# First gate weights on ScalarE's queue, and where the opening transposes of a fused attention and gated-MLP kernel stand

## The chip, the cores and the metric

The kernel runs on one core of one Trainium2 chip. The metric is the device time of one execution in microseconds. The profile's own span, from its first to its last instruction, is about 1.8 us shorter.

## The reference

With x of 2048 rows and 640 columns, everything in bfloat16:

```python
xn = _layernorm(x, axis=-1)
s = _A_ref(xn, A_k_cache, A_v_cache, A_wq, A_wo)   # 32 heads of 192, attention over the last 512 cached keys
g = _silu(_B_ref(xn, B_w_gate, B_w_up, B_w_down))  # (sigmoid(xn @ w_gate) * (xn @ w_up)) @ w_down, inner width 1536
return x + s * g
```

The change touches the first 20 us only: the normalisation of the first four row tiles (128 rows each) and the first four of the twelve column blocks of w_gate (wg) and w_up (wu).

## The kernel before

These are the parts that the change and the argument touch. VectorE computes a tile's statistics and normalises it. TensorE transposes it into PSUM in five blocks of 128 columns, and ScalarE copies the blocks into `xnT`. Only then can TensorE multiply that tile by the weights. Each PSUM buffer, `bank[i]`, is 128 x 2 x 512 float32, so 4 KiB per partition.

```python
bank = [psum.tile([P, 2, 512], F32, name=f"bank{i}") for i in range(4)]
# ... (cut)
        nc.vector.memset(warm[:], 0.0)
        load_x(0, 1)                                  # all loads on SyncE's queue
        load_x(1, 1)
        for f0, f1 in ((0, 4), (4, 8), (8, NF)):
            load_f(nc.sync, wg_sb, wg_r, f0, f1)
            load_f(nc.sync, wu_sb, wu_r, f0, f1)
            if f0 == 0:
                load_x(2, 1)
                load_x(3, 1)
# ... (cut)
        def stats_end(t):
            # ... (cut)
            if t == 0:
                nc.scalar.activation(rstd[:], mv[:, 1:2], AF.Sqrt, bias=eps_t[:], scale=1.0)
                nc.scalar.activation(junk[:], eps_t[:], AF.Sigmoid)
                stats_half(1, 0)                      # needs row tile 1, before row tile 0 is finished
                nc.vector.reciprocal(rstd[:], rstd[:])
# ... (cut)
        def turn_pe(t, c0, c1, bk, eng):
            pT = bk[:, 0:NCD * H2].bitcast(BF16).rearrange("p (c n) -> p c n", c=NCD)
            for c in range(c0, c1):
                nc.tensor.transpose(pT[:, c, :], ln[t][:, c * P:(c + 1) * P], ident[:])
            dst = xnT[:, 0, c0:c1, t * P:(t + 1) * P]
            if eng is nc.vector:
                nc.vector.tensor_copy(dst, pT[:, c0:c1, :])
            else:
                nc.scalar.activation(dst, pT[:, c0:c1, :], AF.Copy)
# ... (cut)
        def tile_gates(t, amid):                      # four groups of wg, then four of wu, five matmuls each
            # ... (cut)
            k = t % 3
            for half, w in ((0, wg_sb), (1, wu_sb)):
                for f in range(FT):
                    if (half, f) == (1, 2) and amid is not None:
                        turn_pe(amid, 0, NCD, bank[3][:, amid % 2, :], nc.scalar)
                    for c in range(NCD):
                        nc.tensor.matmul(bank[k][:, half, f * P:(f + 1) * P],
                                         lhsT=w[:, c, f * P:(f + 1) * P], rhs=xnT[:, 0, c, r],
                                         start=(c == 0), stop=(c == NCD - 1))
            # ... sigmoid on ScalarE, product on VectorE (cut)
# ... (cut)
        dummy(20)                                     # matmuls on zeros, while x is on its way
        full_stats(0)
        normal(0, ((0, 3 * P), (3 * P, D)))
        turn_pe(0, 0, 3, bank[3][:, 0, :], nc.vector)
        turn_pe(0, 3, NCD, bank[2][:, 0, :], nc.scalar)
        dummy(2)
        stats_half(1, 1)
        stats_end(1)
        normal(1)
        full_stats(2)
        tile_gates(0, 1)
        normal(2)
        full_stats(3)
        tile_gates(1, 2)
        normal(3)
        tile_gates(2, 3)
        tile_gates(3, None)
```

The softmax here doesn't subtract the row's maximum and nothing guards it: scores larger than these inputs give would overflow.

Of the kernel before, what the change touches and what calls it, by code (L numbers as in the profile page):

```python
# [8 lines left out]
AF = mybir.ActivationFunctionType  # L9
ALU = mybir.AluOpType  # L10
BF16 = mybir.dt.bfloat16
# [4 lines left out]
def kernel(  # L16
# [13 lines left out]
    nc = tc.nc  # L30
    P = 128
    H2 = 64
# [16 lines left out]
    NCD = D // P  # L49
    NF = F // P  # L50
# [19 lines left out]
    bank = [psum.tile([P, 2, 512], F32, name=f"bank{i}") for i in range(4)]  # L70
# [4 lines left out]
    ident = const.tile([P, P], BF16, name="ident")  # L75
# [5 lines left out]
    xnT = pers.tile([P, NB, NCD, TB], BF16, name="xnT")  # L81
# [5 lines left out]
    wg_r = B_w_gate.rearrange("(c p) f -> p c f", p=P)  # L87
    wu_r = B_w_up.rearrange("(c p) f -> p c f", p=P)
# [45 lines left out]
    with ExitStack() as bctx:  # L134
# [5 lines left out]
        wg_sb = wB.tile([P, NCD, F], BF16, name="wg_sb")  # L140
        wu_sb = wB.tile([P, NCD, F], BF16, name="wu_sb")
# [4 lines left out]
        def load_x(t, n):  # L146

            x = xpool.tile([P, n, D], BF16, name=f"x_sb{n}", bufs=4 if n == 1 else 2)
            nc.sync.dma_start(x[:], xf[t * P:(t + n) * P, :].rearrange("(q p) d -> p q d", p=P))  # L149
            for i in range(n):  # L150
                xt[t + i] = x[:, i, :]

        def load_f(eng, w, r, f0, f1):
            eng.dma_start(w[:, :, f0 * P:f1 * P], r[:, :, f0 * P:f1 * P])  # L154

        nc.vector.memset(warm[:], 0.0)
        load_x(0, 1)
        load_x(1, 1)
        for f0, f1 in ((0, 4), (4, 8), (8, NF)):
            load_f(nc.sync, wg_sb, wg_r, f0, f1)  # L160
            load_f(nc.sync, wu_sb, wu_r, f0, f1)
            if f0 == 0:
                load_x(2, 1)
                load_x(3, 1)
        load_x(TQ, TQ)
        nc.sync.dma_start(wd_sb[:], wd_r)
        load_x(2 * TQ, TQ)
# [7 lines left out]
        def dummy(n):  # L175
            for _ in range(n):
                nc.tensor.matmul(bank[2][:, 1, 0:256], lhsT=warm[:, 0:P], rhs=warm[:, 0:256],
                                 start=True, stop=True)

        ln = {}  # L180

        def stats_half(t, i):
            if i == 0:
                ln[t] = bwork.tile([P, 2, nc.vector.BN_STATS_DIM], F32, name="st")
            nc.vector.bn_stats(ln[t][:, i, :], xt[t][:, i * (D // 2):(i + 1) * (D // 2)])

        def stats_end(t):
            mv = bwork.tile([P, nc.vector.BN_AGGR_DIM], F32, name="mv")
            rstd = bwork.tile([P, 1], F32, name="rstd")
            nc.vector.bn_aggr(mv[:], ln[t][:])  # L190
# [3 lines that stand above are left out]
                stats_half(1, 0)  # L194
                nc.vector.reciprocal(rstd[:], rstd[:])
            else:
                nc.vector.tensor_scalar(rstd[:], mv[:, 1:2], eps, None, op0=ALU.add)
                nc.gpsimd.tensor_tensor(rstd[:], rstd[:], mhalf[:], ALU.pow)
            ln[t] = mv, rstd

        def normal(t, parts=((0, D),)):
            mv, rstd = ln[t]
            xn = xpool.tile([P, D], BF16, name="xn")
            for d0, d1 in parts:
                nc.vector.tensor_scalar(xn[:, d0:d1], xt[t][:, d0:d1], mv[:, 0:1], rstd[:, 0:1],
                                        op0=ALU.subtract, op1=ALU.mult)
            ln[t] = xn

        def turn_pe(t, c0, c1, bk, eng):
            pT = bk[:, 0:NCD * H2].bitcast(BF16).rearrange("p (c n) -> p c n", c=NCD)  # L210
            for c in range(c0, c1):
                nc.tensor.transpose(pT[:, c, :], ln[t][:, c * P:(c + 1) * P], ident[:])  # L212
            dst = xnT[:, 0, c0:c1, t * P:(t + 1) * P]
            if eng is nc.vector:
                nc.vector.tensor_copy(dst, pT[:, c0:c1, :])
            else:
                nc.scalar.activation(dst, pT[:, c0:c1, :], AF.Copy)  # L217

        def turn_dma(t):
            q = t % TQ  # L220
# [2 lines left out]
        hT = {}  # L223
# [41 lines left out]
        FT = 4  # L265

        def tile_gates(t, amid):

            if 0 not in hT:
                hT[0] = hpool.tile([P, NF, TB], BF16, name="hT")  # L270
            k = t % 3
            r = slice(t * P, (t + 1) * P)
            for half, w in ((0, wg_sb), (1, wu_sb)):
                for f in range(FT):
                    if (half, f) == (1, 2) and amid is not None:
                        turn_pe(amid, 0, NCD, bank[3][:, amid % 2, :], nc.scalar)
                    for c in range(NCD):
                        nc.tensor.matmul(bank[k][:, half, f * P:(f + 1) * P],  # L278
                                         lhsT=w[:, c, f * P:(f + 1) * P], rhs=xnT[:, 0, c, r],
                                         start=(c == 0), stop=(c == NCD - 1))  # L280
            sig = bwork.tile([P, TB], BF16, name="sig")
            nc.scalar.activation(sig[:], bank[k][:, 0, :], AF.Sigmoid)
            nc.vector.tensor_tensor(hT[0][:, 0:FT, r],
                                    bank[k][:, 1, :].rearrange("p (f n) -> p f n", f=FT),
                                    sig[:].rearrange("p (f n) -> p f n", f=FT), ALU.mult)

        def full_stats(t):
            stats_half(t, 0)
            stats_half(t, 1)
            stats_end(t)  # L290

        dummy(20)
        full_stats(0)
        normal(0, ((0, 3 * P), (3 * P, D)))
        turn_pe(0, 0, 3, bank[3][:, 0, :], nc.vector)
        turn_pe(0, 3, NCD, bank[2][:, 0, :], nc.scalar)
        dummy(2)
        stats_half(1, 1)
        stats_end(1)
        normal(1)  # L300
        full_stats(2)
        tile_gates(0, 1)
        normal(2)
        full_stats(3)
        tile_gates(1, 2)
        normal(3)
        tile_gates(2, 3)
        tile_gates(3, None)
        k = 1
        for f in range(FT, NF):  # L310
            gated(0, f, k, norm_piece(1, f - FT))
            k = (k + 1) % 4
        for b in range(1, NB):
            for f in range(2):
                gated(b, f, k)
                k = (k + 1) % 4
            for q in range(TQ):
                down(b - 1, q, k)
                k = (k + 1) % 4
            if b == 1:  # L320
                load_x(3 * TQ, TQ)
            for f in range(2, NF):
                gated(b, f, k, norm_piece(b + 1, f - 4) if b + 1 < NB and f >= 4 else None)
                k = (k + 1) % 4
# [4 lines left out]
        for q in range(TQ):  # L329
            down(NB - 1, q, k)  # L330
            k = (k + 1) % 4
# [12 lines left out]
        for m in range(DJ):  # L344
# [3 lines left out]
            k = (k + 1) % 4  # L348
# [168 lines left out]
```

## Time and profile before

| quantity | value |
|---|---|
| time, median of 3 runs | 931.99 us (931.9 to 932.08) |
| span of the profiled run | 930.2 us |
| first gate matmul | 6.94 us |
| first wu matmul | 8.69 us |
| first 512-column gate matmul (end of the opening) | 18.53 us |

In the views PE is TensorE, PEld its weight loads, DVE is VectorE and ACT is ScalarE. The first view is the table of stretches: for each stretch, its length, then the busy time and the number of instructions of PE, PEld, DVE, ACT and POOL (GpSimd), TensorE's granted clock, the busy share of the DMA engines and GB/s.

```profile
7.00:18.50 11.50, 10.33 (x176) 9.79 (x175) 5.79 (x15) 3.58 (x6) 1.67 (x3) 1.00 1.09 353
18.50:915.00 896.50, 896.50 (x7765) 527.11 (x7763) 447.14 (x696) 297.25 (x318) 123.92 (x142) 1.00 0.36 77
```

TensorE is busy through the whole stretch from 18.5 to 915 us. So nothing that the change does before 18.5 us can hide later: the end of the kernel moves with the end of the opening.

The second view is the timeline of TensorE's matmuls: start, length, line, result and operands, how often, and in brackets the idle time before it and what ended it. A matmul of 128 columns is shown 0.22 us long (the profile models where a matmul ends), but the next one starts 0.056 us later. So a gap is read from start to start: a group of 20 fills 1.12 us.

```profile
5.43 0.74 PE L212 MATMUL bank<-ident,xn 128*128 128x128 bf16 x5
...
6.94 1.28 PE L278 MATMUL bank<-xnT,wg_sb 128*128 128x128 bf16 x20
8.69 0.73 PE L278 MATMUL bank<-xnT,wu_sb 128*128 128x128 bf16 x10 [0.47 <-DMA wu_sb<-in_B_w_up_dram]
9.25 0.44 PE L212 MATMUL bank<-ident,xn 128*128 128x128 bf16 x5
9.53 0.72 PE L278 MATMUL bank<-xnT,wu_sb 128*128 128x128 bf16 x10
10.49 1.28 PE L278 MATMUL bank<-xnT,wg_sb 128*128 128x128 bf16 x20 [0.23 <-ACT xnT L217]
...
18.53 1.24 PE L231 MATMUL bank<-xnT,wg_sb 128*128 128x512 bf16 x5
```

The group of 20 that starts at 6.94 has issued its last matmul by 8.06, and wu starts at 8.69. So 0.64 us is lost to the landing of wu. The second ten of wu start at 9.53, and the next tile at 10.49 and not at 10.09: 0.40 us from start to start is lost to the copy of the five transposed blocks (0.36 us by the weight loads). The weight loads show the same gaps more plainly, since each is shown only 0.10 us long. This is the view of waits for them between 6.9 and 18.6 us: total, times, longest. "issue" means that a load stood behind a matmul that waited.

```profile
PEld L278 <- issue: 1.1, 3, 0.4
PEld L278 <- DMA wu_sb<-in_B_w_up_dram: 0.6, 1, 0.6
```

### The profile page before, as it was taken

The numbers are of one execution on the slowest core, as the hardware profiler recorded it, in microseconds if no ns is written. First come the engines' busy times: TensorE is split into PE (matmuls) and PEld (weight loads), VectorE is DVE, ScalarE is ACT, GpSimd is POOL, SyncE is SP. The second block draws the span as 40 slices with busy tenths as digits, with TensorE's granted clock in tenths as the row PEclk, the third lists the DMA queues.
The fourth block names the chain that finished last, engine by engine and source line by source line (L and its number), as shares of the span: only waits on it lengthen the run. The fifth ranks groups of instructions, "written<-read, shape, count | busy, mean of one in ns | idle before, by whom it ended". The sixth has DMA issues, their size and how long they took to land.

```text
span 930.2 us, 18111 instructions
## 1 busy us (share of the span) xinstructions
PE 922.3 (99%) x8036; PEld 546.3 (59%) x8036; DVE 467.5 (50%) x738; ACT 304.5 (33%) x330; POOL 126.5 (14%) x154
## 2 busy tenths in 40 slices
PE   8999999999999999999999999999999999999997
PEld 6445455566655666655566655566666666666665
DVE  5452522454544544554554455445555555445657
ACT  3222222433333333333333333333333333333341
POOL 1000010400010002000200020002000205565000
PEclk9999999999999999999999999999999999999999
DMA  9310420616223433433343433263327234522223
GB/s 314 83 22 8 112 61 1 195 36 138 59 52 78 105 83 61 77 83 99 67 78 58 122 69 78 54 127 69 78 47 133 69 69 78 92 63 63 52 65 102
DMA packets 157807, 76.69 MB, mean 82 GB/s; under 512 B 140784, under 2 KB 151648, under 8 KB 157728
## 3 DMA queue, kind: packets, MB, share of 16 engines
q1 hardware_dynamic: 149904, 46.56, 25.4%
q0 software_dynamic: 7248, 28.38, 10.8%
q8 instruction: 63, 1.03, 0.5%
q10 hardware_dynamic: 576, 0.59, 0.2%
q14 instruction: 16, 0.13, 0.1%
HBM read 39.45 MB, written 2.62 MB: 45 GB/s over the span
## 4 chain that ended last, share of the span: by engine, by line
PE 97%; DVE 1%; DMA 1%; ACT 0%; SPq 0%; issue 0%; DVEq 0%
PE bank L390 22%; PE bank L427 21%; PE bank L407 19%; PE bank L372 18%; PE bank L231 10%; PE bank L243 6%; PE bank L278 1%; DMA wu_sb<-in_B_w_up_dram 1%; PE bank L340 1%; DVE gate L436 1%; DVE o_sb L431 1%; ACT xnT L217 0%; PE bank L212 0%; SPq L149 0%; SPq L154 0%
## 5 line engine op out<-in xcount | busy, mean ns | idle before, releaser
L376 ACT ACTIVATE E<-bank 128x1024 bf16<-128x1024 f32 x256 | 257.9, 1023 | 477.4 <-PE bank L372 453.5
L390 PE MATMUL bank<-xnT,wq_sb 64*128 64x512 bf16 x1860 | 231.4, 376 | 0.0
L427 PE MATMUL bank<-wo_sb,oT 128*128 128x512 bf16 (+1 forms) x1536 | 228.6, 299 | 0.0
L372 PE MATMUL bank<-qT,kT 64*128 64x512 bf16 x1536 | 202.2, 377 | 0.0
L407 PE MATMUL bank<-vbuf,E 128*128 128x193 bf16 x2048 | 191.0, 247 | 0.0
L407 PEld LDWEIGHTS <-E 128*128 128x128 bf16 x2048 | 167.8, 98 | 24.2 <-issue 13.6
L397 DVE CAST qT<-bank 128x1024 bf16<-128x1024 f32 x93 | 113.9, 1224 | 132.8 <-PE bank L390 132.8
L427 PEld LDWEIGHTS <-oT 128*128 128x128 bf16 x1536 | 121.1, 98 | 76.9 <-issue 0.4
L390 PEld LDWEIGHTS <-wq_sb 64*128 64x128 bf16 x1860 | 97.2, 100 | 104.6
L372 PEld LDWEIGHTS <-kT 64*128 64x128 bf16 x1536 | 72.9, 94 | 90.1 <-issue 8.8
L413 DVE TENSOR_TENSOR o_st<-bank,rden 128x768 bf16<-128x768 f32 x128 | 122.5, 957 | 4.4
L442 DVE TENSOR_TENSOR acc<-bank,acc 128x640 f32<-128x640 f32 x96 | 79.1, 824 | 43.8 <-PE bank L427 43.8
L395 DVE COPY seen<-bank 128x2 f32<-128x2 f32 x93 | 14.8, 159 | 93.9 <-PE bank L390 93.8
L412 DVE RECIPROCAL rden<-bank 128x4 f32<-128x4 f32 x128 | 23.3, 182 | 71.4 <-PE bank L407 71.4
L231 PE MATMUL bank<-xnT,wg_sb 128*128 128x512 bf16 x220 | 54.7, 379 | 0.0
L231 PE MATMUL bank<-xnT,wu_sb 128*128 128x512 bf16 x220 | 54.7, 379 | 0.0
L243 PE MATMUL bank<-wd_sb,hT 128*128 128x512 bf16 (+1 forms) x384 | 52.8, 299 | 0.0
L237 DVE TENSOR_TENSOR hT<-bank,sig 128x512 bf16<-128x512 f32 x44 | 30.3, 689 | 43.7 <-ACT sig L234 43.7
L234 ACT ACTIVATE sig<-bank 128x512 bf16<-128x512 f32 x44 | 26.3, 597 | 68.4 <-PE bank L231 63.8
L106 POOL DMA_DIRECT2D vbuf<-in_A_v_cache_dram x28 | 20.9, 748 | 184.9 <-PE bank L407 184.9
L243 PEld LDWEIGHTS <-hT 128*128 128x128 bf16 x384 | 29.6, 98 | 23.2
L231 PEld LDWEIGHTS <-wu_sb 128*128 128x128 bf16 x220 | 21.5, 98 | 26.0
(50 smaller groups left out, 277.6 us busy)
## 6 DMA issues: line engine op xcount, KB each, us to landing
wo_sb<-in_A_wo_dram POOLq DMA_DIRECT2D x8, 960.0 KB, 7.4
wq_sb<-in_A_wq_dram POOLq DMA_DIRECT2D x7, 960.0 KB, 6.3
k_st<-in_A_k_cache_dram POOLq DMA_DIRECT2D x7, 768.0 KB, 8.0
vbuf<-in_A_v_cache_dram POOLq DMA_DIRECT2D x28, 192.0 KB, 3.0
row<-in_A_x_dram POOLq DMA_DIRECT2D x16, 160.0 KB, 2.6
oT<-o_st SPq DMA_TRANSPOSE x128, 2.6
wg_sb<-in_B_w_gate_dram SPq DMA_DIRECT2D x3, 640.0 KB, 7.4
wu_sb<-in_B_w_up_dram SPq DMA_DIRECT2D x3, 640.0 KB, 8.5
```

Of the source, the lines that this page charges most:

```text
L231: nc.tensor.matmul(bank[k][:, half, 0:r1 - r0], lhsT=w[:, c, f * P:(f + 1) * P], rhs=xnT[:, b, c, r0:r1], start=(c == 0), stop=(c == NCD - 1))
L234: nc.scalar.activation(sig[:, 0:r1 - r0], bank[k][:, 0, 0:r1 - r0], AF.Sigmoid)
L237: nc.vector.tensor_tensor(hT[b][:, f, r0:r1], bank[k][:, 1, 0:r1 - r0], sig[:, 0:r1 - r0], ALU.mult)
L243: nc.tensor.matmul(wide(k)[:, d0:d1], lhsT=hT[b][:, f, q * P:(q + 1) * P], rhs=wd_sb[:, f, d0:d1], start=(f == 0), stop=(f == NF - 1))
L372: nc.tensor.matmul(bank[k][:, i, :], lhsT=kT[r, pr, j, c * P:(c + 1) * P], rhs=q[r, pr * DJ + j, :], start=(j == 0), stop=(j == DJ - 1))
L376: nc.scalar.activation(E[u, pr][:, c, :, :], bank[k][:], AF.Exp, scale=scale_qk)
L390: nc.tensor.matmul(bank[k][:, half, :], lhsT=wq[r, c, col:col + DJ * (P - 1) + 1:DJ], rhs=xnT[r, b, c, :], start=(c == 0 and not second), ...
L397: nc.vector.tensor_copy(qT[u][:, 2 * m:2 * m + 2, :], bank[k][:])
L407: nc.tensor.matmul(o4[:, q, 0:DH + 1], lhsT=e[:, c, h % 2, q * P:(q + 1) * P], rhs=v[:, h, c, 0:DH + 1], start=(c == 0), stop=(c == KC - 1))
L413: nc.vector.tensor_tensor(o_st[u][:, :, h * DH:(h + 1) * DH], o4[:, :, 0:DH], rden[:].to_broadcast([P, TQ, DH]), ALU.mult)
L427: nc.tensor.matmul(wide(k)[:, d0:d1], lhsT=oT[u][:, cc, q * P:(q + 1) * P], rhs=wo[:, cc, d0:d1], start=(cc == 0), stop=(cc == GC - 1))
L442: nc.vector.tensor_tensor(acc[:, t, :], wide(k)[:, 0:D], acc[:, t, :], ALU.add)
```

## The change

The change means to bring the first weights sooner and to shorten the waits for copies. wg goes on ScalarE's queue, beside three rows of x on SyncE's. A clear of two of its columns makes that load wait for VectorE. The transposes of a tile stand later, before the last one or two groups of wu. They leave PSUM in two parts (three blocks, then two), both on ScalarE. The statistics of tiles 2 and 3 move forward on VectorE, and each of these tiles is normalised before the gate product that it used to follow. There are 22 dummy matmuls for 20. The diff, cut to its core:

```diff
         nc.vector.memset(warm[:], 0.0)
+        nc.vector.memset(wg_sb[:, 0, 0:2], 0.0)
         load_x(0, 1)
         load_x(1, 1)
-        for f0, f1 in ((0, 4), (4, 8), (8, NF)):
+        load_x(2, 1)
+        load_f(nc.scalar, wg_sb, wg_r, 0, 4)
+        load_f(nc.sync, wu_sb, wu_r, 0, 4)
+        load_x(3, 1)
+        for f0, f1 in ((4, 8), (8, NF)):
             load_f(nc.sync, wg_sb, wg_r, f0, f1)
             load_f(nc.sync, wu_sb, wu_r, f0, f1)
-            if f0 == 0:
-                load_x(2, 1)
-                load_x(3, 1)
# ... (cut)
-        def turn_pe(t, c0, c1, bk, eng):
+        def turn_pe(t):
+            engs = (nc.vector, nc.scalar) if t == 0 else (nc.scalar, nc.scalar)
+            for i, (c0, c1) in enumerate(((0, 3), (3, NCD))):
+                bk = bank[3][:, t % 2, :] if t or i == 0 else bank[2][:, 0, :]
# ... transposes c0 to c1 into bk, then one copy of them by engs[i] (cut)
# ... in tile_gates(t, amid): (cut)
-                    if (half, f) == (1, 2) and amid is not None:
-                        turn_pe(amid, 0, NCD, bank[3][:, amid % 2, :], nc.scalar)
+            for f in range(FT):
+                if amid == f:
+                    turn_pe(t + 1)
+                one(1, wu_sb, f, 0, NCD)
# ... (cut)
-        dummy(20)
-        full_stats(0)
+        dummy(22)
+        stats_half(0, 0)
+        stats_half(0, 1)
+        stats_end(0)
         normal(0, ((0, 3 * P), (3 * P, D)))
-        turn_pe(0, 0, 3, bank[3][:, 0, :], nc.vector)
-        turn_pe(0, 3, NCD, bank[2][:, 0, :], nc.scalar)
+        turn_pe(0)
         dummy(2)
         stats_half(1, 1)
         stats_end(1)
+        stats_half(2, 0)
         normal(1)
-        full_stats(2)
-        tile_gates(0, 1)
+        stats_half(2, 1)
+        stats_end(2)
+        stats_half(3, 0)
+        stats_half(3, 1)
         normal(2)
-        full_stats(3)
-        tile_gates(1, 2)
+        stats_end(3)
+        m0 = tile_gates(0, 3)                          # m0() is the product on VectorE
+        m0()
         normal(3)
-        tile_gates(2, 3)
-        tile_gates(3, None)
+        m1 = tile_gates(1, 2)
+        m1()
+        m2 = tile_gates(2, 2)
+        m2()
+        m3 = tile_gates(3, None)
+        m3()
```

More of the change, by code (lines that the diff above doesn't have):

```diff
@@ L207, in normal @@
             ln[t] = xn
-        def turn_pe(t, c0, c1, bk, eng):
-            pT = bk[:, 0:NCD * H2].bitcast(BF16).rearrange("p (c n) -> p c n", c=NCD)
-            for c in range(c0, c1):
-                nc.tensor.transpose(pT[:, c, :], ln[t][:, c * P:(c + 1) * P], ident[:])
-            dst = xnT[:, 0, c0:c1, t * P:(t + 1) * P]
-            if eng is nc.vector:
-                nc.vector.tensor_copy(dst, pT[:, c0:c1, :])
-            else:
-                nc.scalar.activation(dst, pT[:, c0:c1, :], AF.Copy)
+        def turn_pe(t):
+            engs = (nc.vector, nc.scalar) if t == 0 else (nc.scalar, nc.scalar)
+            for i, (c0, c1) in enumerate(((0, 3), (3, NCD))):
+                bk = bank[3][:, t % 2, :] if t or i == 0 else bank[2][:, 0, :]
+                pT = bk[:, 0:NCD * H2].bitcast(BF16).rearrange("p (c n) -> p c n", c=NCD)
+                for c in range(c0, c1):
+                    nc.tensor.transpose(pT[:, c, :], ln[t][:, c * P:(c + 1) * P], ident[:])
+                dst = xnT[:, 0, c0:c1, t * P:(t + 1) * P]
+                if engs[i] is nc.vector:
+                    nc.vector.tensor_copy(dst, pT[:, c0:c1, :])
+                else:
+                    nc.scalar.activation(dst, pT[:, c0:c1, :], AF.Copy)
         def turn_dma(t):
@@ L272, in tile_gates, with one @@
             r = slice(t * P, (t + 1) * P)
-            for half, w in ((0, wg_sb), (1, wu_sb)):
-                for f in range(FT):
-                    if (half, f) == (1, 2) and amid is not None:
-                        turn_pe(amid, 0, NCD, bank[3][:, amid % 2, :], nc.scalar)
-                    for c in range(NCD):
-                        nc.tensor.matmul(bank[k][:, half, f * P:(f + 1) * P],
-                                         lhsT=w[:, c, f * P:(f + 1) * P], rhs=xnT[:, 0, c, r],
-                                         start=(c == 0), stop=(c == NCD - 1))
+            def one(half, w, f, c0, c1):
+                for c in range(c0, c1):
+                    nc.tensor.matmul(bank[k][:, half, f * P:(f + 1) * P],
+                                     lhsT=w[:, c, f * P:(f + 1) * P], rhs=xnT[:, 0, c, r],
+                                     start=(c == 0), stop=(c == NCD - 1))
+            for f in range(FT):
+                one(0, wg_sb, f, 0, NCD)
+            for f in range(FT):
+                if amid == f:
+                    turn_pe(t + 1)
+                one(1, wu_sb, f, 0, NCD)
             sig = bwork.tile([P, TB], BF16, name="sig")
             nc.scalar.activation(sig[:], bank[k][:, 0, :], AF.Sigmoid)
-            nc.vector.tensor_tensor(hT[0][:, 0:FT, r],
-                                    bank[k][:, 1, :].rearrange("p (f n) -> p f n", f=FT),
-                                    sig[:].rearrange("p (f n) -> p f n", f=FT), ALU.mult)
-        def full_stats(t):
-            stats_half(t, 0)
-            stats_half(t, 1)
-            stats_end(t)
-        dummy(20)
-        full_stats(0)
+            return lambda: nc.vector.tensor_tensor(
+                hT[0][:, 0:FT, r], bank[k][:, 1, :].rearrange("p (f n) -> p f n", f=FT),
+                sig[:].rearrange("p (f n) -> p f n", f=FT), ALU.mult)
+        dummy(22)
+        stats_half(0, 0)
+        stats_half(0, 1)
+        stats_end(0)
         normal(0, ((0, 3 * P), (3 * P, D)))
-        turn_pe(0, 0, 3, bank[3][:, 0, :], nc.vector)
-        turn_pe(0, 3, NCD, bank[2][:, 0, :], nc.scalar)
+        turn_pe(0)
         dummy(2)
```

## The prediction

> **What bounds the kernel.** TensorE. The table of stretches shows it busy for 896.50 of 896.50 us between 18.5 and 915 us, and the chain of waits is 97% TensorE. The change touches only what stands before 18.53 us, where (timeline) the first 512-column gate matmul starts. All that follows should move with that instant, one to one.
>
> **The opening now** (timeline, waits): x lands at 3.06, statistics, square root and normalising take until 5.2, transposes start at 5.43, the copies out of PSUM end at 6.59, the first gate matmul starts at 6.94. Then 160 matmuls of 128 columns and 15 transposes, 56 ns each. Idle between: 0.64 us for the first wu (landed 8.64), and three times about 0.36 us, where a tile's first matmul waits for ScalarE's 0.70 us copy of its transposed rows, which two groups of wu matmuls (0.56 us) hide in part. So at most 1.7 us can be won after 6.94.
>
> **What the change does.**
> 1. Queues. wg goes out on ScalarE's queue at about 1.2 instead of 1.67 us, beside three rows of x. The transfers ran at 350 GB/s from 4 us on, and a 655 KB weight took 1.87 us. The Trainium skill ("DMA: Bandwidth & Descriptors", Issuing engines are not separate DMA queues) says that both queues run on the same 16 DMA engines and interleave; so only the earlier start counts, half a microsecond, and x row 2 takes 0.46 us ahead of wu. Estimate: wu about 0.4 us earlier, wg about as before (6.8).
> 2. 22 dummy matmuls for 20. They run cold, 213 ns apart, from 1.19 us; the 20th ends just as the normalised row is ready (5.13). Two more delay transposes, copies and gates by up to 0.43 us; estimate 0.36. The wu wait then vanishes.
> 3. Late transposes, two copies on ScalarE. Both parts of a tile share one PSUM bank, and the built program makes the fourth transpose wait for the first copy. The skill's "PSUM — Partial Sum Buffer" (PSUM bank collisions raise a hardware error) has why: TensorE may not write a bank that another engine reads. The trace of before has no such case. From 0.38 us for 256 columns and 0.70 for 640, a 384-column copy takes 0.49 us (estimate). Three transposes, 0.26 us to the copy's start, copy, restart: TensorE stands about 0.73 us in the middle of each tile's transposes. Afterwards the second copy is hidden for tiles 2 and 3, where two groups follow; for tile 1 one follows, and 0.2 us more is waited. So 0.73+0.73+0.93 us against 3 x 0.36: 1.3 us lost.
> 4. Statistics of rows 2 and 3 earlier on VectorE: off the path.
>
> **Sum.** +0.36 (start) +1.3 (stalls) -0.64 (wu) = about +0.9 us: first 512-column matmul near 19.4 us, span 931.1, time 932.8 us. Range 931.2 to 933.9. Chances: faster by over 2% 0.004, within 2% 0.991, slower 0.005.
>
> **What would show each step right.** Timeline: first transposes near 5.85, first gate near 7.3, no idle for wu; in each of three transposes a TensorE gap of about 0.7 us after the third, released by ScalarE's copy; ScalarE copies 0.49 and 0.38 us; first 512-column matmul at 19.4; then no TensorE gap until the tail.
>
> **What would make it wrong.** If the clock rises during the extra dummies, the start is not delayed, and the loss is 0.5. If the two queues delay row 0 or row 1 of x, or wg lands after 7.3, the start slips further.  If the fourth transpose's wait overlaps more than I count, the change could gain up to 0.7 us.

## The result

| | before | changed |
|---|---|---|
| time, median of 4 runs of the same rounds | 932.04 us (931.9 to 932.2) | 932.93 us (932.87 to 933.22) |
| span of the profiled run | 930.2 us | 931.2 us |
| first transposes | 5.43 us | 5.86 us |
| first gate matmul | 6.94 us | 7.29 us |
| first wu matmul | 8.69 us | 8.47 us |
| first 512-column gate matmul | 18.53 us | 19.54 us |
| from first wu to first 512-column matmul | 9.84 us | 11.07 us |

A ratio is the mean time of one kernel's fast runs over that of the other's of the same rounds, so it is not quite the ratio of these medians. It is 1.001, with a 95% interval of 0.9993 to 1.0028. On the interval alone the slowdown of 0.9 us isn't resolved, though the four runs of each kernel do not overlap. The traces settle where it comes from: the opening ends 1.01 us later.

In the table of stretches of the changed kernel TensorE is again busy for all of the time after its opening (896.40 of 896.40 us). The opening is what grew. Its busy time there says little, since the modelled end of a matmul covers the beginning of each gap.

```profile
7.00:19.40 12.40, 10.56 (x175) 9.98 (x175) 6.00 (x17) 4.33 (x10) 1.67 (x3) 1.00 1.08 354
19.40:915.80 896.40, 896.40 (x7765) 527.26 (x7763) 446.88 (x696) 297.25 (x318) 123.92 (x142) 1.00 0.35 77
```

This is the timeline of its matmuls over the first two tiles and at the end of the opening, with the same columns.

```profile
5.86 0.74 PE L219 MATMUL bank<-ident,xn 128*128 128x128 bf16 x5
...
7.29 1.28 PE L283 MATMUL bank<-xnT,wg_sb 128*128 128x128 bf16 x20
8.47 1.01 PE L283 MATMUL bank<-xnT,wu_sb 128*128 128x128 bf16 x15
9.32 0.33 PE L219 MATMUL bank<-ident,xn 128*128 128x128 bf16 x3
10.23 0.27 PE L219 MATMUL bank<-ident,xn 128*128 128x128 bf16 x2 [0.58 <-ACT xnT L224]
10.34 0.44 PE L283 MATMUL bank<-xnT,wu_sb 128*128 128x128 bf16 x5
10.62 1.47 PE L283 MATMUL bank<-xnT,wg_sb 128*128 128x128 bf16 x20
...
19.54 1.24 PE L238 MATMUL bank<-xnT,wg_sb 128*128 128x512 bf16 x5
```

Three transposes start at 9.32. The other two start at 10.23, when ScalarE has finished its copy of the first three. TensorE does nothing between. The copies are these, in the timeline of ScalarE:

```profile
9.69 0.49 ACT L224 ACTIVATE xnT<-bank 128x384 bf16<-128x384 bf16 x1 [2.67 <-PE bank L219]
10.54 0.38 ACT L224 ACTIVATE xnT<-bank 128x256 bf16<-128x256 bf16 x1 [0.36 <-PE bank L219]
```

The weight loads between 6.9 and 19.6 us, against 1.1 us in three waits and 0.6 us for wu in before:

```profile
PEld L219 <- issue: 2.1, 3, 0.7
```

That is three gaps of 0.70 us inside the transposes (0.74 from start to start of the matmuls). After the first tile there is a little more: the 20 matmuls from 10.62 take 1.47 us and not 1.28, because those that need blocks 3 and 4 wait for the second copy. The sum is (2.1 + 0.2) - 1.1 = 1.2 us, and 11.07 less 9.84 is 1.23.

### The profile page after: what moved, and what is told of

Read it like the earlier page. It is cut to its first block, busy times and chain, and to the rows that moved or that the text cites. A ratio compares the mean times of both kernels' runs of the same rounds, so it can differ in the third digit from the quotient of the medians.

```text
span 931.2 us, 18119 instructions
## 1 busy us (share of the span) xinstructions
PE 922.8 (99%) x8038; PEld 546.8 (59%) x8038; DVE 467.3 (50%) x739; ACT 305.2 (33%) x333; POOL 126.5 (14%) x154
## 4 chain that ended last, share of the span: by engine, by line
PE 98%; DVE 1%; ACT 0%; issue 0%; DVEq 0%
PE bank L406 22%; PE bank L443 21%; PE bank L423 19%; PE bank L388 18%; PE bank L238 10%; PE bank L250 6%; PE bank L283 1%; PE bank L356 1%; DVE gate L452 1%; DVE o_sb L447 1%; PE bank L180 1%; PE bank L219 0%; ACT xnT L224 0%; DVEq L528 0%; DVE warm L156 0%
```

## The experiments

The main theory: the built program makes the fourth transpose wait for the first copy, and TensorE, which takes its work in order, stands still. That costs 1.2 us; queues and dummies matter little. The rivals: the second queue or the later start costs the time; the gap is only the old wait in another place; or the late place of the transposes costs it.

The landing of wu moved between runs by up to 0.6 us (first wu matmul 8.38 to 9.01), so the interval from the first wu matmul to the first 512-column matmul is the better measure. Before and changed were profiled once each, and the experiments in three later sessions on three chips, each beside runs of before; comparisons of times with the changed kernel therefore go across sessions. In the traces of e1, e2 and e3 the record of the first 512-column matmul is missing, so it is taken from its weight load plus the 0.05 us that lie between the two in before.

| run | what | time, us (runs) | before beside it | first wu | first 512-column | interval |
|---|---|---|---|---|---|---|
| before | | 932.04 (4) | | 8.69 | 18.53 | 9.84 |
| changed | | 932.93 (4) | 932.04 | 8.47 | 19.54 | 11.07 |
| e1 | before + queues | 932.07 (4) | 931.97 | 8.40 | 18.24 | 9.84 |
| e2 | before + 22 dummies | 932.13 (4) | 931.97 | 8.97 | 18.81 | 9.84 |
| e3 | before + late, two copies | 933.60 (4) | 931.97 | 8.82 | 20.23 | 11.41 |
| e4 | changed, two banks | 933.37 (4) | 931.97 | 8.79 | 19.86 | 11.07 |
| f1 | changed, two buffers | 931.59 (4) | 932.09 | 9.00 | 18.47 | 9.47 |
| f2 | changed, one copy | 932.02 (4) | 932.09 | 8.40 | 18.53 | 10.13 |
| f3 | one copy, early, 20 dummies | 930.72 (5) | 932.09 | 9.01 | 17.79 | 8.78 |
| f4 | changed, no clear | 935.56 (1, state unknown) | 932.09 | 10.81 | 22.08 | 11.27 |
| g1 | changed, 20 dummies | 932.85 (4) | 932.23 | 8.38 | 19.44 | 11.06 |
| g2 | f4 again | 935.05 (4) | 932.23 | 10.54 | 21.60 | 11.06 |

### e1: the new order of loads alone

```diff
 (before, with the loads and the clear of the changed kernel; nothing else)
+        nc.vector.memset(wg_sb[:, 0, 0:2], 0.0)
+        load_f(nc.scalar, wg_sb, wg_r, 0, 4)
```

> The kernel before with only the new order of loads (wg on ScalarE's queue behind a 2-column clear of its tile; x rows 0, 1, 2, then wu, then x row 3 on SyncE's). First 512-column gate matmul: 18.53 us in before, 19.54 in the changed kernel. Main theory (the loss is the wait between two copies out of one PSUM bank): the queues help by the earlier wu alone, which then starts near 8.47 instead of 8.69 us; the start slips by about 0.15 us (row 0 of x landed at 3.19 instead of 3.04) inside the remaining wu wait. First 512-column matmul 18.3 us, time 0.2 us shorter than before. Rival (the second queue disturbs the loads and costs the time): first 512-column matmul at 18.9 us or later, time 0.4 us longer or more.

The first 512-column matmul came at 18.24 us, as the main theory had it, and the interval was that of before. The times don't show the 0.2 us: 932.07 against 931.97, with single runs from 931.62 to 933.98. So the queues don't cost the microsecond; that they win anything rests on this one trace.

### e2: 22 dummies alone

```diff
-        dummy(20)
+        dummy(22)
```

> The kernel before with 22 dummy matmuls for 20, nothing else. First transposes 5.86 instead of 5.43 us, first gate matmul 7.29 instead of 6.94. Main theory: wu still lands near 8.64, so its wait shrinks from 0.64 to about 0.3 us and takes up the whole delay: first 512-column matmul 18.5 us, time unchanged within 0.1 us. Rival (the delay of the start passes through to the end): 18.9 us, time 0.36 us longer.

The time did not change (932.13 against 931.97). The run did not test the step as meant, though. The spacing of the dummies fell from 213 to 110 ns at about 4.0 us: TensorE's clock had risen. In the changed kernel the transposes as late as 6.2 us still stood 107 ns apart (56 ns for such matmuls later on), at the low clock, and in before those at 5.8 us. So the 22 dummies were over sooner, and the first transposes started at 5.20, not 5.86. The later end (18.81 against the expected 18.5) is wholly the landing of wu, 0.28 us later; the interval is 9.84 us. g1 takes this up.

### e3: late transposes and two copies alone

```diff
-                    if (half, f) == (1, 2) and amid is not None:
-                        turn_pe(amid, 0, NCD, bank[3][:, amid % 2, :], nc.scalar)
+                    if half == 1 and f == amid:
+                        turn_pe(t + 1)                 # two parts, as in the changed kernel
# ... and tile_gates(0, 3), tile_gates(1, 2), tile_gates(2, 2)
```

> The kernel before with only the new transposes: two copies on ScalarE from one bank, the first tile's transposes one group later. Queues, dummies and order of statistics as before. Main theory: three gaps of 0.74 us after the third transpose and 0.2 us more after the first tile: first 512-column matmul 19.75 us (18.53 plus 1.3, less the few hundredths by which the split spares the start of the copy), time 1.2 us longer than before. Rival (the gap is the old wait of 0.36 us only moved, and the loss comes from queues and dummies): 18.5 to 18.8 us, time within 0.3 us.

This part alone makes the kernel 1.6 us slower (933.60 against 931.97; ratio 1.0023, 0.6 to 4.0 thousandths), and the interval 11.41 us. The theory's 1.2 us is there, and 0.34 us more, which it had not counted. The view of weight loads shows both, the latter in its third line: they wait for normalised rows as well, on VectorE.

```profile
PEld L216 <- issue: 2.1, 3, 0.7
PEld L282 <- DMA wu_sb<-in_B_w_up_dram: 0.7, 1, 0.7
PEld L216 <- DVE xn L205: 0.3, 1, 0.3
```

With before's order on VectorE, tile 3 is normalised behind the product of tile 1. The sigmoid for that product started at 14.68 us: it had waited for TensorE, which the gap had held up, and not for the two copies (the second ended at 14.50). The changed kernel's order normalises tile 3 before that product, at 12.05 us against 15.92 in e3, and there the wait is absent. So the new order does work, but only against a delay that the new transposes bring. This is read from two traces; no run changes that order alone.

### e4: the two parts in two banks of one buffer

```diff
-                bk = bank[3][:, t % 2, :] if t or i == 0 else bank[2][:, 0, :]
+                bk = bank[3][:, i, :] if t or i == 0 else bank[2][:, 0, :]
```

> The changed kernel with one edit: the two parts of a tile's transposes lie in two PSUM banks (the two halves of the same buffer, both free by then). Main theory: the gap between the third and fourth transpose is gone (five transposes 56 ns apart), and what is left is a wait of the next tile's matmuls for the copies, about 0.3, 0.3 and 0.6 us: first 512-column matmul near 18.3 us, time about 1.2 us shorter than the changed kernel and 0.2 to 0.3 us shorter than before. Rival: no more than 0.3 us won, first 512-column matmul 19.2 us or later.

This failed: the interval is the changed kernel's to the hundredth, and the gap is still there in the timeline (three transposes, two transposes, then the next group):

```profile
9.64 0.33 PE L219 MATMUL bank<-ident,xn 128*128 128x128 bf16 x3
10.55 0.27 PE L219 MATMUL bank<-ident,xn 128*128 128x128 bf16 x2 [0.58 <-ACT xnT L224]
10.66 0.44 PE L283 MATMUL bank<-xnT,wu_sb 128*128 128x128 bf16 x5
```

Looking at the built program explains it: the fourth transpose still waits for the count that the first copy raises. The two parts lie 2 KiB apart, but in one buffer, `bank[3]`, and the program was built with waits between the users of a buffer. So the edit took no wait away. It refutes the reason that I had given for the wait in this build, not the wait.

### f1: the two parts in two buffers

```diff
-                bk = bank[3][:, t % 2, :] if t or i == 0 else bank[2][:, 0, :]
+                bk = bank[3][:, t % 2, :] if i == 0 else bank[2][:, 0, :] if t == 0 else bank[(t + 1) % 3][:, 1, :]
```

> The changed kernel with one edit: the second part of a tile's transposes goes to another PSUM buffer altogether (not the other bank of the same buffer, where e4 still waited). Measured from the start of the wu matmuls, because the landing of wu moved by 0.3 us between runs: to the first 512-column gate matmul it took 9.84 us in before, 11.07 in the changed kernel and 11.07 in e4. Theory (the built program waits by buffer; with that wait gone only the wait for the copies at the next tile is left, about 0.3, 0.3 and 0.6 us): 9.8 us, no gap between third and fourth transpose, time 1.2 us shorter than the changed kernel. Rival (the gap is the hardware's switch from a copy to transposes, or the two copies themselves cost it): 10.7 us or more.

With the second part in another buffer the five transposes follow on one another, and the next tile waits for the first copy, 0.35 us from start to start (0.19 in the view, which counts from the modelled end):

```profile
9.85 0.44 PE L219 MATMUL bank<-ident,xn 128*128 128x128 bf16 x5
10.13 0.44 PE L283 MATMUL bank<-xnT,wu_sb 128*128 128x128 bf16 x5
10.76 1.38 PE L283 MATMUL bank<-xnT,wg_sb 128*128 128x128 bf16 x20 [0.19 <-ACT xnT L224]
```

The interval falls from 11.07 to 9.47 us, 0.3 us more than expected, and the time to 931.59 us, 1.3 us below the changed kernel of the earlier session and 0.5 below before (ratio 0.9995, interval 0.998 to 1.001, so this last isn't resolved). The kernel still has two copies, still on ScalarE, still late. In the built program its fourth transpose has no wait for ScalarE. So neither the copies nor a switch of TensorE makes the gap: the wait does. The interval is even 0.37 us shorter than that of before.

### f2: one copy, late

```diff
-            for i, (c0, c1) in enumerate(((0, 3), (3, NCD))):
+            for i, (c0, c1) in enumerate(((0, 3), (3, NCD)) if t == 0 else ((0, NCD),)):
```

> The changed kernel with one edit: one copy of all five transposes on ScalarE, as in before, at the changed kernel's late places. Theory: no gap inside the transposes; the next tile waits 0.36, 0.36 and, after the first tile where one group less hides the copy, 0.65 us. From the start of the wu matmuls to the first 512-column matmul 10.05 us (before 9.84, changed 11.07): the two copies cost about 1.0 us and the later place 0.3 us. Rival (lateness costs most): 10.7 us or more.

The interval was 10.13 us (expected 10.05). So from one buffer two copies cost 0.94 us over one, and the later place of the first tile's transposes costs 0.29 us (10.13 less 9.84). Together they are the 1.23 us.

### f3: the version that these point to

```diff
-            for i, (c0, c1) in enumerate(((0, 3), (3, NCD))):
+            for i, (c0, c1) in enumerate(((0, 3), (3, NCD)) if t == 0 else ((0, NCD),)):
-        dummy(22)
+        dummy(20)
-        m0 = tile_gates(0, 3)
+        m0 = tile_gates(0, 1)
-        m1 = tile_gates(1, 2)
+        m1 = tile_gates(1, 0)
-        m2 = tile_gates(2, 2)
+        m2 = tile_gates(2, 0)
```

> The version that the experiments point to: the changed kernel with one copy, 20 dummies, and the transposes earlier (after one group of wu in the first tile, before all of them in the next two), so that three or four groups hide the copy. Theory: waits of about 0.1 us after the first tile and none after the others; from the start of the wu matmuls to the first 512-column matmul 8.8 us, that matmul at 17.2 to 17.5 us (18.53 in before), time 1.0 to 1.4 us shorter than before, ratio 0.9988. Rival (VectorE has the rows too late for early transposes): 9.5 us or more.

The interval was 8.78 us (expected 8.8). With four groups of wu between the transposes and the next tile, one copy is hidden whole: between wu at 11.93 and wg at 13.04 there is no gap, and the transposes at 11.65 follow the group of 20 at once. With three groups, after the first tile, 0.12 us is left (wu from 9.58 to 10.42, wg at 10.54).

```profile
9.01 0.45 PE L283 MATMUL bank<-xnT,wu_sb 128*128 128x128 bf16 x5 [0.61 <-DMA wu_sb<-in_B_w_up_dram]
9.30 0.44 PE L219 MATMUL bank<-ident,xn 128*128 128x128 bf16 x5
9.58 1.00 PE L283 MATMUL bank<-xnT,wu_sb 128*128 128x128 bf16 x15
10.54 1.28 PE L283 MATMUL bank<-xnT,wg_sb 128*128 128x128 bf16 x20
11.65 0.44 PE L219 MATMUL bank<-ident,xn 128*128 128x128 bf16 x5
11.93 1.28 PE L283 MATMUL bank<-xnT,wu_sb 128*128 128x128 bf16 x20
13.04 1.28 PE L283 MATMUL bank<-xnT,wg_sb 128*128 128x128 bf16 x20
```

wu landed late in this run (it was waited for until 9.01), so the first 512-column matmul came at 17.79 and not by 17.5 us. The time is 930.72 us against 932.09 for before: ratio 0.9987, interval 0.9974 to 0.9999. It is the fastest of all kernels here.

### f4 and g2: without the clear of two columns

```diff
-        nc.vector.memset(wg_sb[:, 0, 0:2], 0.0)
```

> The changed kernel without the 2-column clear of wg's tile, which makes ScalarE's load wait until 1.14 us: wg then is issued at about 0.74 us, together with row 0 of x. If the clear is there to keep wg from row 0 of x: row 0 lands later than 3.05 to 3.2 us, by 0.3 us or more, and the statistics start as much later. If it is of no use: row 0 lands within 0.15 us of 3.19 and wg about 0.4 us earlier. From the start of the wu matmuls on nothing differs (11.07 us).

> The same kernel as f4 (changed kernel without the clear of two columns), timed, because f4 was one look of unknown state. There row 1 of x landed at 6.24 instead of 3.88 us, behind the whole of wg, and the normalising of row 0, which stands behind row 1's statistics on VectorE, came 2 us late. If that is what the clear prevents: row 1's first statistics at 5.5 us or later, all runs 2 to 3 us longer than the changed kernel's 932.9 us. If f4 was an accident: 933 us.

The clear is of use, but for row tile 1 and not for row tile 0 as f4's expectation had it. In f4 the statistics of tile 0 started at 3.37 us and those of tile 1 at 6.26. The timed repeat shows the same, here in VectorE's timeline:

```profile
3.49 0.89 DVE L187 BATCH_NORM_STATS2 st<-x_sb 128x6 f32<-128x320 bf16 x2 [2.34 <-DMA x_sb<-in_A_x_dram]
4.41 0.21 DVE L192 BATCH_NORM_AGGREGATE mv<-st 128x2 f32<-128x12 f32 x1
5.83 0.49 DVE L187 BATCH_NORM_STATS2 st<-x_sb 128x6 f32<-128x320 bf16 x1 [1.22 <-DMA x_sb<-in_A_x_dram]
6.25 0.15 DVE L197 RECIPROCAL rstd<-rstd 128x1 f32<-128x1 f32 x1
```

VectorE waited 1.22 us for row tile 1, and tile 0's reciprocal stands behind it in VectorE's order. The opening ended 2.06 us later than in the changed kernel, and the time was 935.05 us, 2.1 us longer than the changed kernel's of the first session. Only about half of that is the late tile itself: the first transposes started 1.00 us later (6.86 against 5.86). The other half is TensorE's clock. Here the 20 wg matmuls of the first tile stand 107 ns apart, the spacing of the low clock, and last until wu starts at 10.54, though wu had landed at 8.51. In the changed kernel they stand 56 ns apart and take 0.99 us less. These are g2's matmuls:

```profile
6.86 0.71 PE L218 MATMUL bank<-ident,xn 128*128 128x128 bf16 x5 [0.79 <-DVE xn L207]
8.05 0.58 PE L179 MATMUL bank<-warm 128*128 128x256 bf16 x2 [0.47 <-ACT xnT L223]
8.43 2.28 PE L282 MATMUL bank<-xnT,wg_sb 128*128 128x128 bf16 x20
10.54 1.00 PE L282 MATMUL bank<-xnT,wu_sb 128*128 128x128 bf16 x15
```

The loads explain the late tile. Tile 1's load was issued at 1.20 us on SyncE's queue, wg at 0.74 on ScalarE's, and tile 1 landed at 5.81 us, after wg (5.36). The clear puts wg's issue at 1.19 us, and tile 1 then landed at 3.88. (In f1, with the clear, it landed at 4.84 and delayed the first transposes to 5.89 us; wu, landing at 8.95, hid that.)

### g1: the changed kernel with 20 dummies

```diff
-        dummy(22)
+        dummy(20)
```

> The changed kernel with 20 dummy matmuls for 22, nothing else. The prediction held the two extra dummies for a delay of 0.36 us at the start. But in e2, f1, f2 and f4 the clock rose during the dummies (near 4.1 to 4.4 us), and 22 of them were over by 5.3. Theory now (the number of dummies moves the first gate matmul only where the clock is still low, and wu's landing, 8.4 to 9.0 us, takes up what it moves): first gate matmul at 6.7 to 7.1 us, wu matmuls still at 8.4 to 9.0, from there to the first 512-column matmul 11.07 us as in the changed kernel, time within 0.3 us of it. Rival (the two dummies cost 0.36 us as predicted): wu matmuls near 8.1 us, 0.3 us shorter than the changed kernel.

The first gate matmul started 0.65 us earlier than in the changed kernel (6.64 against 7.29), and it was worth next to nothing: wu matmuls could start at 8.38 and not before, since wu landed at 8.33 (8.47 and 8.43 in the changed kernel). The time was 932.85 against 932.93 us. Here too the clock rose during the dummies, near 4.3 us, so how much of the 0.65 us belongs to the number of dummies is not separated.

## Why the prediction was right

- **The total.** Predicted 932.8 us and 19.4 us for the first 512-column matmul; measured 932.93 and 19.54. The prediction's terms as written (+0.36, +1.3, -0.64) add up to 1.02 and not to its 0.9; the measured shift was 1.01.
- **One to one.** Right: the opening ended 1.01 us later, and the span grew by 1.0 us, with no TensorE gap until the tail.
- **The wait inside the transposes.** Right in place, releaser and size: three gaps of 0.70 us by the weight loads, 0.74 by the matmuls (predicted 0.73), copies of 0.49 and 0.38 us, 1.23 us in all (predicted 1.3). e3 brings it with the transposes alone, f1 takes it away by the buffer alone, and f2 by one copy.
- **The reason for that wait.** Not right as given. I had drawn on the Trainium skill, "PSUM — Partial Sum Buffer" (PSUM bank collisions raise a hardware error), which forbids TensorE and another engine the same bank at once. In the changed kernel both parts do share a bank, so by that page the wait could not have been left out there; no run tests this. But e4, with the parts 2 KiB apart (one bank each, by the size that the page states), kept the same gap of 0.70 us. What this build waits by is the buffer.
- **Queues.** Too large in size, and the direction isn't shown: wu landed at 8.43 and not 8.64 us in this pair of traces, so 0.2 us earlier where I said 0.4. But with the new queues it landed anywhere from 8.33 to 8.96 (seven traces), with the old from 8.64 to 8.92 (three).
- **The dummies.** The trace of the changed kernel agreed: 22 of them at the low clock, transposes at 5.86, first gate matmul at 7.29, no wait for wu left to speak of (0.06 us). But the prediction's sum counted +0.36 for the start and -0.64 for wu as two terms. They are one: the wu matmuls start at the later of two instants. That start moved by -0.22 us (8.69 to 8.47), which is nearly the same net of -0.28. The dummies' delay was not on the critical path by more than about 0.1 us: in the changed trace wu landed at 8.43 just as the gate matmuls ended (8.41), and g1 started 0.65 us sooner for nothing. That the start came out at 7.29 was partly luck: of seven traces with 22 dummies the clock stayed low to their end in three (changed, e4, g2) and rose before it in four (e2, f1, f2, f4). The prediction's warning that a risen clock would cut the loss to 0.5 was not borne out by g1: the clock rose there, and the opening still ended at 19.44.
- **Statistics off the path.** Right for the changed kernel, but by e3's trace another 0.34 us would have been lost without the new order.

## What to carry to other kernels

Splitting a copy out of PSUM so that its reader can start sooner works only if the writer need not wait between the parts. Put the parts in separate buffers, look in the built program for a wait inside the writing group, and remember that an in-order engine stands still there. Where there is other work to put between writing and reading, writing earlier hides a whole copy and is simpler than splitting it. A start that is made earlier is worth only what the next arrival leaves: here the first gate matmul moved by 0.65 us and the end by 0.1, about as much as wu happened to land earlier.

## What the Trainium skill lacked or had wrong

- "PSUM — Partial Sum Buffer": it states the rule by bank. No page says that a built program may wait by whole buffer: with the two parts 2 KiB apart in one 4 KiB buffer, TensorE stood 0.70 us between the third and fourth transpose of each tile (e4); in two buffers it did not (f1).
- "DMA: Bandwidth & Descriptors" (Issuing engines are not separate DMA queues) says that loads of several engines interleave, and that several issuing engines save only issue time. The runs don't contradict it, but the section has no figure for what an earlier large load costs a small one. Here a 655 KB load issued at 0.74 us on ScalarE's queue landed at 5.36 us, and a 164 KB load issued at 1.20 on SyncE's queue only after it, at 5.81 (g2; f4: 5.78 and 6.24). With the large one issued at 1.19 us the small one landed at 3.88 (changed) to 4.84 (f1). So the issue time that was saved cost the first transposes 1.0 us. Why the small load came last is not shown.
- "TensorE: Matmul & The Clock Gate" (The HAM clock gate) gives about 4 us of sustained work, give or take 0.5 us, before the clock rises. With matmuls back to back from 1.19 us on, it rose 2.8 us after the first of them in e2 (at 4.0 us), and in the changed kernel it was still low 5.0 us after it (at 6.2 us). That is a wider spread than the page states. The page puts the spread down to a window that runs free of the kernel's start; no run here tests that.
